# First chunk normed and turned tile by tile, mask copies on VectorE, and six output tiles moved among the second exp units

## The chip, the cores and the metric

The kernel runs on one core of a Trainium2 chip. The metric is device time in microseconds (us), as the median of several executions. The time is longer than the span of the profile, which runs from the first to the last instruction: by 1.8 us in the kernel before.

Engines are named as the profile names them: PE (TensorE matmul), PEld (its weight loads), DVE (VectorE), ACT (ScalarE), POOL (GpSimd), SP (SyncE). "SPq" is SyncE's queue, used here for DMA issues. L640 is line 640 of that kernel's own file, so one operation has different line numbers in different kernels.

## The reference, cut to what matters

```python
x = A_x                                    # 1 x 2048 x 512, bf16
xn = layernorm(x)
# branch A: 32 heads of 16, each query sees 8 keys at distance 0, 2, .., 14
qkv = xn @ wqkv;  attn = softmax(mask(q . k / 4));  s = (attn . v) @ wo
# branch B: LN, w1, gelu, shift in time by group, w2, residual, LN, w3, gelu, w4, residual
h  = gelu(layernorm(xn) @ w1);  x1 = xn + shift(h) @ w2
b  = x1 + gelu(layernorm(x1) @ w3) @ w4
out = x + s * silu(b)
```

Since the distances are even, even and odd tokens are two separate problems of 1024 tokens ("parity" p = 0, 1).

## The kernel before

Each parity is cut into nine attention units of up to 128 queries. The program has five stages:

1. The head: layer norm of four chunks of 512 tokens, their transposes, most q/k products and all w1 products.
2. The nine units of parity 0, filled with q/k and w2 products.
3. All of w3.
4. The nine units of parity 1, filled with w4 tiles.
5. The tail: the remaining w4 tiles, the gates, and 16 output tiles called `final_tile`.

Program order is issue order on each engine. These are the parts that the change and the argument touch.

```python
wm = psa("warm_ps")                        # warm-up of PE
for i in range(16):
    nc.tensor.matmul(wm[:, i % 2, :], lhsT=ones_bf[:], rhs=..., start=True, stop=True)
...
def mask_diag():                           # three column sums by VectorE
    nc.vector.tensor_tensor(out=tab[:, :, 0:P], in0=tab[:, :, 0:P], in1=ident..., op=ALU.mult)
    nc.vector.tensor_reduce(out=mg[:, 0:3], in_=tab[:, :, 0:P], ...)
def mask_rows():  ...                      # nine small operations, all on GpSimd
def mask_wide():  ...                      # two copies of 128x1024 on ScalarE
def mask_turn():                           # 2 x 16 matmuls of 64 columns, two copies on ScalarE
    ...
def mask_fill(k):                          # the mask into the queries and keys: four DMAs of 512 KB
    cs = slice(k * CH, (k + 1) * CH)
    for w in range(2):
        for e in range(2):
            nc.sync.dma_start(
                out=(kT, qT)[w][e][:, :, cs], in_=mask[:, w, cs].unsqueeze(1).to_broadcast([P, ND, CH]))
...
def rsqrt_eps(dst, var):                   # the inverse root of every layer norm: on GpSimd
    nc.gpsimd.tensor_scalar(out=dst, in0=var, scalar1=EPS, scalar2=None, op0=ALU.add)
    nc.gpsimd.tensor_tensor(out=dst, in0=dst, in1=nhalf[:, 0 : dst.shape[-1]], op=ALU.pow)
...
def final_tile(p, i, eng=nc.vector):
    pt = psa("wo_ps")[:, 0, :]
    for dt in range(ND):
        nc.tensor.matmul(pt, lhsT=oT[p][:, dt, i * P : (i + 1) * P], rhs=wo_sb[:, dt, :], ...)
    ...
    nc.vector.tensor_tensor(out=sg, in0=pt, in1=xn[p][:, i, :], op=ALU.mult)     # L638
    x_o = xo[p][:, i, :]
    eng.tensor_tensor(out=x_o, in0=sg, in1=x_o, op=ALU.add)                      # L640
...
    load_w3()
    va = values(0, 0)                      # value product of the first unit
    stage_w1(3, 0)
    stage_w1(3, 1)                         # last gelus, then ScalarE loads its exp table
...
    for n in range(N1, 2 * NU):            # nine units of parity 1, with w4 tiles 0 to 9
        attend(n)
    ...
    for t in range(10, 16):                # tail
        w4s[t](0, NF)
        final_tile(*fq.pop(0), eng=nc.gpsimd)
        gate(t)
        ...
    for _ in range(2):
        final_tile(*fq.pop(0), eng=nc.gpsimd)
    ...
    for i in range(8):
        final_tile(1, i, eng=nc.vector if i % 2 else nc.gpsimd)
        if i % 2:
            store(nc.scalar, 1, i - 1)
        if i == 2:
            normalise_end(1, 2)
```

The softmax here doesn't subtract the row's maximum and nothing guards it: scores larger than these inputs give would overflow.

Of the kernel before, what the change touches and what calls it, by code (L numbers as in the profile page):

```python
# [15 lines left out]
def kernel(  # L16
# [153 lines left out]
    def mask_tables():  # L170
        gp = nc.gpsimd
        for i, o, v in ((0, 0, -7), (0, 15, 8), (1, 1, -7), (1, 16, 7)):
            gp.iota(
                tab[:, i, o : o + 135].rearrange("p (k t) -> p k t", t=15)[:, ::2],
                pattern=[[0, 5], [1 if o < 15 else -1, 15]], base=v, channel_multiplier=0,
                allow_small_or_imprecise_dtypes=True,
            )
        gp.memset(tab[:, 1, 0:1], -8.0)
        gp.iota(
            tab[:, 2, 0:P].rearrange("p (g k) -> p g k", k=2), pattern=[[0, P // 2], [-2, 2]], base=1,  # L180
            channel_multiplier=0, allow_small_or_imprecise_dtypes=True,
        )
        for w in range(2):
            m = rows[w]
            gp.memset(m, 0.0)
            gp.memset(m[:, :, 3:11], PEN if w == 0 else 0.0)
            gp.affine_select(
                out=m[:, :, 3:11], in_=m[:, :, 3:11], pattern=[[-1, W], [1, W]],
                compare_op=ALU.is_ge if w == 0 else ALU.not_equal,
                fill=-PEN if w == 0 else 1.0, base=0, channel_multiplier=0,  # L190
            )
        gp.memset(rows[0][:, :, 2], -PEN)
        gp.memset(rows[1][:, :, 0], 1.0)

    def mask_diag():
        nc.vector.tensor_tensor(
            out=tab[:, :, 0:P], in0=tab[:, :, 0:P], in1=ident.unsqueeze(1).to_broadcast([P, 3, P]), op=ALU.mult
        )
        nc.vector.tensor_reduce(out=mg[:, 0:3], in_=tab[:, :, 0:P], axis=mybir.AxisListType.X, op=ALU.add)

    def mask_rows():
        gp = nc.gpsimd
        sg, q = mg[:, 2:3], mg[:, 3:4]
        one = ones_bf[:, 0:W]
        for w in range(2):
            m = rows[w]
            c, d = mg[:, w : w + 1], m[:, :, 3:11]
            gp.tensor_scalar(out=d, in0=d, scalar1=sg, scalar2=None, op0=ALU.mult)
            gp.tensor_scalar(out=q, in0=c, scalar1=-1.0 if w == 0 else 1.0, scalar2=c, op0=ALU.add, op1=ALU.mult)
            if w == 0:  # L210
                gp.tensor_scalar(out=q, in0=q, scalar1=1.0, scalar2=-PEN, op0=ALU.add, op1=ALU.mult)
                gp.tensor_scalar(out=m[:, :, 0], in0=one, scalar1=q, scalar2=None, op0=ALU.mult)
                gp.tensor_scalar(out=m[:, :, 1], in0=one, scalar1=c, scalar2=2 * PEN, op0=ALU.mult, op1=ALU.mult)
            else:
                gp.tensor_scalar(out=m[:, :, 1], in0=one, scalar1=c, scalar2=None, op0=ALU.mult)
                gp.tensor_scalar(out=m[:, :, 2], in0=one, scalar1=q, scalar2=None, op0=ALU.mult)

    def mask_wide():
        for w in range(2):
            nc.scalar.copy(  # L220
                out=wide[:, w, :].rearrange("p (l n r) -> p l n r", l=W, r=16),
                in_=rows[w].unsqueeze(2).to_broadcast([P, W, P // 16, 16]),
            )

    def mask_turn():
        for w in range(2):
            pt = psa("mask_ps").rearrange("p b x -> p (b x)")
            pv = pt.rearrange("p (b g l) -> p b l g", b=2, l=W)
            for b in range(2):
                for l in range(W):  # L230
                    nc.tensor.matmul(
                        pv[:, b, l, :], lhsT=wide[:, w, l * P : (l + 1) * P], rhs=ident[:, b * 64 : b * 64 + 64],
                        start=True, stop=True,
                    )
            nc.scalar.copy(out=mask[:, w, :], in_=pt)

    def mask_fill(k):
        cs = slice(k * CH, (k + 1) * CH)
        for w in range(2):
            for e in range(2):  # L240
                nc.sync.dma_start(
# [14 lines left out]
    for i in range(NV):  # L256
        va = const.tile([P, H, 2 * DH], BF16, name=f"v_aug{i}")
        nc.gpsimd.memset(va[:, :, DH : 2 * DH], 2.0)
        v_aug.append(va)

# [23 lines left out]
    def ln_stats(c, lo=0, hi=TPC):  # L284
        p, k = c // 2, c % 2
        lns.setdefault(c, []).append((lo, hi, *layer_stats(xn[p][:, k * TPC : (k + 1) * TPC, :], "l1", lo, hi)))

# [341 lines left out]
    def final_tile(p, i, eng=nc.vector):  # L629
        pt = psa("wo_ps")[:, 0, :]  # L630
# [7 lines left out]
        nc.vector.tensor_tensor(out=sg, in0=pt, in1=xn[p][:, i, :], op=ALU.mult)  # L638
# [13 lines left out]
    ln_stats(0, 0, 2)  # L652
    ln_stats(0, 2, 4)
    ln_norm(0)
    stage_t(0, 0)
    stage_t(0, 1)
    ln_again(0)
    mask_diag()
    mask_rows()
    ln_stats(1)  # L660
    ln_again(1)
    stage_d(0)
    ln_norm(1)
    parts = [qk_pair(0, a, 2) for a in range(2)]
    for hh in range(2):
        for f in parts:
            f[hh]()
    mask_wide()
    qk_pair(0, 2)[0]()
    stage_r(0)  # L670
    stage_m(0)
    qk_pair(0, 3)[0]()
    mask_turn()
    mask_fill(0)
    stage_t(1, 0)
    stage_t(1, 1)
    spread(0, 0, CH)
    mask_fill(1)
    ln_stats(2)
    ln_again(2)  # L680
    stage_w1(0, 0)
    stage_w1(0, 1)
    stage_d(1)
    ln_norm(2)
# [6 lines left out]
    spread(0, CH, M)  # L691
    stage_t(2, 0)
    stage_t(2, 1)
    ln_stats(3)
    ln_again(3)
    stage_d(2)
# [11 lines left out]
    stage_m(3)  # L708
    stage_w1(2, 0)
    stage_w1(2, 1)  # L710
    load_w3()
    va = values(0, 0)
    stage_w1(3, 0)
    stage_w1(3, 1)

# [10 lines left out]
    for n, (a, b) in enumerate(  # L726
        (("www", "q"), ("w", "qw"), ("w", "qq"), ("w", "qw"), ("w", "qq"), ("w", "qw"), ("w", "qq"), ("w", "qw"), ("w", "qw"))
# [20 lines left out]
    for n in range(N1, 2 * NU):  # L748
        t = n - N1
        if t == 0:  # L750
            groups[n][0].append(lambda: w4s[0](0, NF))
            groups[n][0].append(lambda: w4s[1](0, 5))
            groups[n][1].append(lambda: w4s[1](5, NF))
        else:
            groups[n][0].append(lambda t=t: gate(t - 1))
            groups[n][0].append(lambda t=t: w4s[t + 1](0, 5))
            groups[n][1].append(lambda t=t: w4s[t + 1](5, NF))
# [19 lines left out]
    def attend(n):  # L777
# [3 lines left out]
        out = weighted(*prev) if prev is not None else None  # L781
        for f in groups[n][0]:
            f()
# [4 lines left out]
        if out and n >= N1:  # L788
            out()
# [12 lines left out]
    for c in range(NCH):  # L802
        for a in range((NF + 1) // 2):
            w3_pair(c, a)
            if c == 0 and a == 0:
# [12 lines left out]
                load_w4()  # L818
                pack(0, 2)
# [6 lines left out]
    load_wo()  # L826
# [10 lines left out]
    fq = [(0, i) for i in range(8)]  # L837
    gate(8)
    gate(9)
    for t in range(10, 16):  # L840
        w4s[t](0, NF)
        final_tile(*fq.pop(0), eng=nc.gpsimd)
        gate(t)
        if t == 11:
            normalise_end(1, 1)
        if t == 13:
            normalise_mid(1, 2)
            normalise_rr(1, 2)
    for _ in range(2):
        final_tile(*fq.pop(0), eng=nc.gpsimd)  # L850
    for i in (0, 2, 4, 6):
        store(nc.sync, 0, i)
    for i in range(8):
        final_tile(1, i, eng=nc.vector if i % 2 else nc.gpsimd)
        if i % 2:
            store(nc.scalar, 1, i - 1)
        if i == 2:
            normalise_end(1, 2)
# [30 lines left out]
```

## Time and profile before

| What | Value | View |
|---|---|---|
| time | 217.96 us (217.96 to 217.99) | timed runs |
| span | 216.2 us | page |
| PE busy | 202.4 us, 94% | page |
| PE stops being the limit | 198.9 us | chain of waits |
| DVE's last add ends | 210.05 us | timeline |
| PE in the last 5 us before 210 | 2.50 of 5 us | table of windows |

First, two lines of the page's second part. Each digit is the busy share of one fortieth of the span.

```profile
PE   8999999999999999999999999999999999999830
POOL 8881505000054797902180000000610708534940
```

PE is full until slice 37. The loss is at the end. The table of windows shows the same place in finer steps: the window, its length, then the busy time of each engine with its number of instructions.

```profile
195.00:200.00 5.00, 4.62 (x21) 2.02 (x21) 4.91 (x5) 0.63 (x1) 2.22 (x2) 1.00 0.54 145
200.00:205.00 5.00, 4.03 (x18) 1.67 (x18) 4.97 (x8) 0.00 (x0) 4.66 (x4) 1.00 0.40 136
205.00:210.00 5.00, 2.50 (x11) 0.88 (x9) 4.90 (x8) 0.00 (x0) 2.84 (x3) 1.00 0.44 150
```

The first busy column is PE and the third is DVE. DVE is full (4.97, 4.90) while PE falls to half. The chain of waits, which is the work that ended last in order of time, agrees.

```profile
203.41 1.12 DVE arena L615
204.53 0.61 DVE arena L638
...
207.86 1.29 DVE arena L638 x2
209.15 0.02 issue
209.17 0.88 DVE arena L640
```

DVE's last add ends at 210.05, yet the span lasts to 216.2. The view of the program's closing line shows why. Its columns are the count, then the shortest, median and longest duration in ns, then the first and last start.

```profile
L884 POOLq DRAIN  x3: 40/102/6513, 208.6 to 215.6; - x3
L884 SPq DRAIN  x3: 7/7/13, 212.4 to 215.4; - x3
```

SyncE starts its closing at 212.4, when the last store has landed. GpSimd's first drain starts at 208.6 and lasts 6.51 us, to 215.1. The closing barrier comes only after that.

### The profile page before, as it was taken

The numbers are of one execution on the slowest core, as the hardware profiler recorded it, in microseconds if no ns is written. First come the engines' busy times: TensorE is split into PE (matmuls) and PEld (weight loads), VectorE is DVE, ScalarE is ACT, GpSimd is POOL, SyncE is SP. The second block draws the span as 40 slices with busy tenths as digits, with TensorE's granted clock in tenths as the row PEclk, the third lists the DMA queues.
The fourth block names the chain that finished last, engine by engine and source line by source line (L and its number), as shares of the span: only waits on it lengthen the run. The fifth ranks groups of instructions, "written<-read, shape, count | busy, mean of one in ns | idle before, by whom it ended". The sixth has DMA issues, their size and how long they took to land.

```text
span 216.2 us, 5001 instructions
## 1 busy us (share of the span) xinstructions
PE 202.4 (94%) x1999; PEld 98.9 (46%) x2028; DVE 132.8 (61%) x242; ACT 133.1 (62%) x162; POOL 78.1 (36%) x155
## 2 busy tenths in 40 slices
PE   8999999999999999999999999999999999999830
PEld 2557455444444444544444444445444444444310
DVE  4868686223788786867731000355667697799980
ACT  2378678859879888665665568788888861211000
POOL 8881505000054797902180000000610708534940
PEclk9999999999999999999999999999999999999995
DMA  5993977977401697772589766880210603105431
GB/s 134 359 349 113 322 110 166 312 115 144 188 5 20 159 171 101 160 171 48 151 200 201 235 128 98 254 264 0 53 33 4 138 15 79 57 0 136 151 115 49
DMA packets 34782, 29.75 MB, mean 138 GB/s; under 512 B 12600, under 2 KB 32408, under 8 KB 34760
## 3 DMA queue, kind: packets, MB, share of 16 engines
q1 hardware_dynamic: 31624, 25.24, 44.2%
q0 software_dynamic: 2048, 3.15, 8.9%
q10 hardware_dynamic: 1088, 1.05, 1.4%
q8 instruction: 16, 0.26, 0.5%
q14 instruction: 6, 0.05, 0.1%
HBM read 12.39 MB, written 4.46 MB: 78 GB/s over the span
## 4 chain that ended last, share of the span: by engine, by line
PE 79%; DVE 5%; ACT 5%; SPq 4%; issue 4%; DMA 1%; DVEq 0%
PE w_ps L458 18%; PE w_ps L478 17%; PE qk_ps L362 7%; PE v_ps L504 6%; PE s_ps L524 6%; PE w_ps L414 5%; SPq L250 4%; PE qk_ps L378 4%; PE o_ps L547 4%; PE wo_ps L632 3%; PE w_ps L391 3%; PE warm_ps L161 3%; DVE arena L638 3%; ACT arena L529 2%; PE tr_ps L314 1%
## 5 line engine op out<-in xcount | busy, mean ns | idle before, releaser
L529 ACT ACTIVATE arena<-s_ps 128x960 bf16<-128x960 f32 (+2 forms) x72 | 63.1, 934 | 15.8 <-PE s_ps L524 15.1
L589 POOL DMA_DIRECT2D arena<-orw x48 | 25.2, 532 | 61.6 <-DVE orw L559 61.6
L478 PE MATMUL w_ps<-arena 128*128 128x512 bf16 (+1 forms) x154 | 38.7, 379 | 0.7 <-issue 0.2
L463 ACT ACTIVATE arena<-w_ps 128x1024 bf16<-128x1024 f32 x20 | 20.5, 1024 | 15.6 <-PE w_ps L458 14.9
L458 PEld LDWEIGHTS <-arena 128*128 128x128 bf16 (+1 forms) x176 | 17.5, 100 | 20.2
L478 PEld LDWEIGHTS <-arena 128*128 128x128 bf16 (+1 forms) x176 | 16.5, 97 | 19.4 <-issue 0.4
L494 DVE SCALAR_TENSOR_TENSOR arena<-sig,arena 128x512 bf16<-128x512 bf16 x16 | 14.7, 926 | 14.2 <-ACT sig L493 14.1
L559 DVE CAST orw<-o_ps 128x960 bf16<-128x960 f32 (+2 forms) x18 | 19.7, 1095 | 1.4 <-PE o_ps L547 1.4
L493 ACT ACTIVATE sig<-arena 128x512 bf16<-128x512 bf16 x16 | 10.1, 630 | 16.2 <-DVE arena L484 16.2
L458 PE MATMUL w_ps<-arena 128*128 128x512 bf16 (+1 forms) x86 | 19.4, 379 | 0.1
L418 DVE TENSOR_TENSOR arena<-w_ps,arena 128x512 bf16<-128x512 f32 x16 | 11.0, 688 | 13.7 <-PE w_ps L414 13.6
L524 PEld LDWEIGHTS <-arena 32*128 32x128 bf16 (+1 forms) x576 | 11.8, 94 | 16.7 <-issue 16.2
L458 PE MATMUL w_ps<-arena,arena 128*128 128x512 bf16 (+1 forms) x86 | 19.1, 379 | 0.1
L640 POOL TENSOR_TENSOR arena<-arena 128x512 bf16<-128x512 bf16 x12 | 14.8, 1244 | 11.6 <-DVE arena L638 11.6
L524 PE MATMUL s_ps<-arena 32*128 32x120 bf16 (+2 forms) x576 | 18.5, 211 | 0.5 <-ACT arena L529 0.2
L504 PE MATMUL v_ps<-wv_sb,arena 128*128 128x512 bf16 (+1 forms) x71 | 18.5, 381 | 0.1
L362 PE MATMUL qk_ps<-arena 128*128 128x512 bf16 (+1 forms) x95 | 18.2, 343 | 0.2
L266 POOL TENSOR_SCALAR l3r<-l3m 128x1 f32<-128x1 f32 (+1 forms) x10 | 2.3, 229 | 41.3 <-DVE l3m L275 41.3
L414 PE MATMUL w_ps<-arena 128*128 128x512 bf16 x55 | 15.6, 381 | 0.6 <-issue 0.2
L508 DVE CAST v_aug<-v_ps 128x512 bf16<-128x512 f32 (+1 forms) x18 | 12.4, 687 | 4.9 <-PE v_ps L504 4.9
L484 DVE TENSOR_TENSOR arena<-w_ps,arena 128x512 bf16<-128x512 f32 x16 | 10.9, 680 | 6.8 <-PE w_ps L478 6.7
L391 PE MATMUL w_ps<-arena 128*128 128x512 bf16 x61 | 14.3, 379 | 0.2
(83 smaller groups left out, 262.7 us busy)
## 6 DMA issues: line engine op xcount, KB each, us to landing
arena<-arena SPq DMA_DIRECT2D x8, 512.0 KB, 5.6
arena<-arena SPq DMA_DIRECT2D x48, 64.0 KB, 2.5
x1n_dram<-arena SPq DMA_DIRECT2D x4, 512.0 KB, 4.3
arena<-in_A_x_dram SPq DMA_DIRECT2D x4, 512.0 KB, 8.0
arena<-in_A_x_dram SPq DMA_DIRECT2D x6, 256.0 KB, 7.0
arena<-in_B_w_dram SPq DMA_DIRECT2D x1, 1376.0 KB
arena<-in_B_w_dram SPq DMA_DIRECT2D x1, 1280.0 KB
arena<-in_A_wqkv_dram SPq DMA_DIRECT2D x2, 512.0 KB, 4.4
```

The lines of the kernel that those rows point to most:

```text
L362: nc.tensor.matmul(pt[:, b, hh * w : (hh + 1) * w], lhsT=wqk_sb[:, dt, nt * P : (nt + 1) * P], rhs=xnT[p][:, dt, k * CH + hh * w : k * CH ...
L391: nc.tensor.matmul(pt[:, b, :], lhsT=w1_sb[:, dt, g * P : (g + 1) * P], rhs=xn2T[c][:, dt, :], start=(dt == 0), stop=(dt == ND - 1),)
L414: nc.tensor.matmul(pt, lhsT=w2_src(p, g, m0), rhs=w2_sb[:, g, :], start=(g == 0), stop=(g == ND - 1))
L458: nc.tensor.matmul(pt[:fs, ft % 2, :], lhsT=w3_sb[:, dt, ft * P : ft * P + fs], rhs=x1nT[c][:, dt, :], start=(dt == 0), stop=(dt == ND - 1),)
L463: nc.scalar.activation(h3(c, 2 * a, 2), pt, AF.Gelu_apprx_tanh)
L478: nc.tensor.matmul(pt, lhsT=h3(c, ft, 1)[:fs, 0, jj * P : (jj + 1) * P], rhs=w4_sb[:fs, ft, :], start=(ft == 0), stop=(ft == NF - 1),)
L504: nc.tensor.matmul(vp[:nk, :], lhsT=xnT[p][:, dt, k0 : k0 + nk], rhs=wv_sb[:, dt, :], start=(dt == 0), stop=(dt == ND - 1),)
L524: nc.tensor.matmul(st[:nk, b, i * nq : (i + 1) * nq], lhsT=kT[e][r : r + 32, dt, k0 : k0 + nk], rhs=qT[e][r : r + 32, dt, q0 : q0 + nq], s ...
L529: nc.scalar.activation(prv[:nk, 2 * h : 2 * h + 2], st[:nk, :, 0 : 4 * nq], AF.Exp, scale=SCALE)
L559: nc.vector.tensor_copy(out=orw[p][:, :, :, q0 - ra : q0 - ra + nq], in_=op[:, :, 0 : 4 * nq].rearrange("p j (s q) -> p j s q", q=nq),)
L589: nc.gpsimd.dma_start(out=oT[p][DH * hh : DH * (hh + 1), :, ra : ra + rw], in_=orw[p][32 * cg : 32 * cg + DH, jj],)
L640: eng.tensor_tensor(out=x_o, in0=sg, in1=x_o, op=ALU.add)
```

## The change

The change has three parts:

- **Head.** Chunk 0 is normed and turned one tile at a time. The mask's column sums move from VectorE to PE, its turn becomes 16 transposes, and its widening and eight copies move from ScalarE and DMA to VectorE. Part of its small operations move from GpSimd to VectorE, and the statistics of chunks 1 and 3 are taken in halves.
- **Units.** The value product of the first unit moves behind the last w1 products, and one more q/k product goes into that unit. Six output tiles of parity 0 move into units 2 and 6 of parity 1, and two fewer w4 tiles are done there.
- **Tail.** Seven of the eight w4 tiles each carry one output tile and three output tiles follow the last w4 tile; all adds of the tail are on VectorE, and the last store is 128 KB.

```diff
+    def mask_cols():                       # replaces mask_diag
+        pt = pst("w", "mask_ps")[:, 0, 0:3]
+        for i in range(3):
+            nc.tensor.matmul(pt[:, i : i + 1], lhsT=tab[:, i, 0:P], rhs=ident[:, 0:1], start=True, stop=True)
+        nc.scalar.copy(out=mg[:, 0:3], in_=pt)
...
+    def mask_turn(w):
+        pt = psa("mask_ps").bitcast(BF16)
+        for l in range(W):
+            nc.tensor.transpose(pt[:, w, l * P : (l + 1) * P], wide[:, w, l * P : (l + 1) * P], ident[:])
...
     def mask_fill(k):
         ...
-                nc.sync.dma_start(
+                nc.vector.tensor_copy(
                     out=(kT, qT)[w][e][:, :, cs], in_=mask[:, w, cs].unsqueeze(1).to_broadcast([P, ND, CH])
...
+    parts = [qk_pair(0, a, 2) for a in range(3)]     # head, in the new order
+    parts[0][0]()
+    ...
+    mask_cols()
+    mask_rows(0, nc.gpsimd)
+    ln_stats(1, 0, 2)
...
+    stage_d(1)
+    mask_fill(0)
+    spread(0, 0, CH)
     ln_norm(2)
...
     load_w3()
-    va = values(0, 0)
     stage_w1(3, 0)
     stage_w1(3, 1)
+    va = values(0, 0)
...
+    fill = {0: (0, 1), 1: (2,), 3: (3,), 4: (4,), 5: (5,), 7: (6,), 8: (7,)}   # w4 tiles by unit
+    rows_of = {2: (0, 1, 2), 6: (3, 4, 5)}                                     # output tiles by unit, adds on GpSimd
...
-    for t in range(10, 16):
+    fq = [(0, 6), (0, 7)] + [(1, i) for i in range(8)]
+    for t in range(8, 16):
         w4s[t](0, NF)
-        final_tile(*fq.pop(0), eng=nc.gpsimd)
...
+        if t < 15:
+            p, i = fq.pop(0)
+            final_tile(p, i, ps=psa)       # add on VectorE
+            gate(t)
...
+    final_tile(1, 5, ps=psa, act=True)     # act: ScalarE copies the product out of PSUM first
+    store(nc.sync, 1, 4)
+    gate(15)
+    final_tile(1, 6, ps=psa, act=True)
+    store(nc.sync, 1, 6, 1)
+    final_tile(1, 7, ps=psa)
+    store(nc.scalar, 1, 7, 1)
```

More of the change, by code (lines that the diff above doesn't have):

```diff
@@ L182, in mask_tables @@
         )
-        for w in range(2):
-            m = rows[w]
-            gp.memset(m, 0.0)
-            gp.memset(m[:, :, 3:11], PEN if w == 0 else 0.0)
-            gp.affine_select(
-                out=m[:, :, 3:11], in_=m[:, :, 3:11], pattern=[[-1, W], [1, W]],
-                compare_op=ALU.is_ge if w == 0 else ALU.not_equal,
-                fill=-PEN if w == 0 else 1.0, base=0, channel_multiplier=0,
-            )
-        gp.memset(rows[0][:, :, 2], -PEN)
-        gp.memset(rows[1][:, :, 0], 1.0)
@@ L195, in mask_diag @@
-    def mask_diag():
-        nc.vector.tensor_tensor(
-            out=tab[:, :, 0:P], in0=tab[:, :, 0:P], in1=ident.unsqueeze(1).to_broadcast([P, 3, P]), op=ALU.mult
-        )
-        nc.vector.tensor_reduce(out=mg[:, 0:3], in_=tab[:, :, 0:P], axis=mybir.AxisListType.X, op=ALU.add)
-    def mask_rows():
-        gp = nc.gpsimd
+    def mask_cols():
[3 more added lines that the diff above has]
+        nc.scalar.copy(out=mg[:, 0:3], in_=pt)
@@ new lines, in mask_forms @@
+    def mask_forms(w):
+        gp = nc.gpsimd
+        m = rows[w]
+        gp.memset(m, 0.0)
+        gp.memset(m[:, :, 3:11], PEN if w == 0 else 0.0)
+        gp.affine_select(
+            out=m[:, :, 3:11], in_=m[:, :, 3:11], pattern=[[-1, W], [1, W]],
+            compare_op=ALU.is_ge if w == 0 else ALU.not_equal,
+            fill=-PEN if w == 0 else 1.0, base=0, channel_multiplier=0,
+        )
+        if w == 0:
+            gp.memset(m[:, :, 2], -PEN)
+        else:
+            gp.memset(m[:, :, 0], 1.0)
@@ L203, in mask_rows @@
+    def mask_rows(w, eng):
         sg, q = mg[:, 2:3], mg[:, 3:4]
         one = ones_bf[:, 0:W]
-        for w in range(2):
-            m = rows[w]
-            c, d = mg[:, w : w + 1], m[:, :, 3:11]
-            gp.tensor_scalar(out=d, in0=d, scalar1=sg, scalar2=None, op0=ALU.mult)
-            gp.tensor_scalar(out=q, in0=c, scalar1=-1.0 if w == 0 else 1.0, scalar2=c, op0=ALU.add, op1=ALU.mult)
-            if w == 0:
-                gp.tensor_scalar(out=q, in0=q, scalar1=1.0, scalar2=-PEN, op0=ALU.add, op1=ALU.mult)
-                gp.tensor_scalar(out=m[:, :, 0], in0=one, scalar1=q, scalar2=None, op0=ALU.mult)
-                gp.tensor_scalar(out=m[:, :, 1], in0=one, scalar1=c, scalar2=2 * PEN, op0=ALU.mult, op1=ALU.mult)
-            else:
-                gp.tensor_scalar(out=m[:, :, 1], in0=one, scalar1=c, scalar2=None, op0=ALU.mult)
-                gp.tensor_scalar(out=m[:, :, 2], in0=one, scalar1=q, scalar2=None, op0=ALU.mult)
+        m = rows[w]
+        c, d = mg[:, w : w + 1], m[:, :, 3:11]
+        eng.tensor_scalar(out=d, in0=d, scalar1=sg, scalar2=None, op0=ALU.mult)
+        eng.tensor_scalar(out=q, in0=c, scalar1=-1.0 if w == 0 else 1.0, scalar2=c, op0=ALU.add, op1=ALU.mult)
+        if w == 0:
+            eng.tensor_scalar(out=q, in0=q, scalar1=1.0, scalar2=-PEN, op0=ALU.add, op1=ALU.mult)
+            eng.tensor_scalar(out=m[:, :, 0], in0=one, scalar1=q, scalar2=None, op0=ALU.mult)
+            eng.tensor_scalar(out=m[:, :, 1], in0=one, scalar1=c, scalar2=2 * PEN, op0=ALU.mult, op1=ALU.mult)
+        else:
+            eng.tensor_scalar(out=m[:, :, 1], in0=one, scalar1=c, scalar2=None, op0=ALU.mult)
+            eng.tensor_scalar(out=m[:, :, 2], in0=one, scalar1=q, scalar2=None, op0=ALU.mult)
@@ L218, in mask_wide @@
     def mask_wide():
         for w in range(2):
-            nc.scalar.copy(
+            nc.vector.tensor_copy(
                 out=wide[:, w, :].rearrange("p (l n r) -> p l n r", l=W, r=16),
@@ L223, in mask_wide @@
             )
-    def mask_turn():
-        for w in range(2):
-            pt = psa("mask_ps").rearrange("p b x -> p (b x)")
-            pv = pt.rearrange("p (b g l) -> p b l g", b=2, l=W)
-            for b in range(2):
-                for l in range(W):
-                    nc.tensor.matmul(
-                        pv[:, b, l, :], lhsT=wide[:, w, l * P : (l + 1) * P], rhs=ident[:, b * 64 : b * 64 + 64],
-                        start=True, stop=True,
-                    )
-            nc.scalar.copy(out=mask[:, w, :], in_=pt)
+    def mask_turn(w):
+        pt = psa("mask_ps").bitcast(BF16)
+        for l in range(W):
+            nc.tensor.transpose(pt[:, w, l * P : (l + 1) * P], wide[:, w, l * P : (l + 1) * P], ident[:])
+        nc.scalar.copy(
+            out=mask[:, w, :].rearrange("p (g l) -> p g l", l=W), in_=pt[:, w, :].rearrange("p (l g) -> p g l", l=W)
+        )
     def mask_fill(k):
@@ L240, in mask_fill @@
             for e in range(2):
-                nc.sync.dma_start(
+                nc.vector.tensor_copy(
                     out=(kT, qT)[w][e][:, :, cs], in_=mask[:, w, cs].unsqueeze(1).to_broadcast([P, ND, CH])
@@ L257, with v_ones @@
         va = const.tile([P, H, 2 * DH], BF16, name=f"v_aug{i}")
-        nc.gpsimd.memset(va[:, :, DH : 2 * DH], 2.0)
         v_aug.append(va)
+    def v_ones():
+        for va in v_aug:
+            nc.gpsimd.memset(va[:, :, DH : 2 * DH], 2.0)
     for p in range(2):
@@ L286, in ln_stats, with ln_first, first_n, first_t @@
         lns.setdefault(c, []).append((lo, hi, *layer_stats(xn[p][:, k * TPC : (k + 1) * TPC, :], "l1", lo, hi)))
+    first = {}
+    def ln_first(j):
+        if not first:
+            first["st"] = small.tile([P, TPC, nc.vector.BN_STATS_DIM], F32, name="l0s", tag="l0s", bufs=1)
+            first["mv"] = small.tile([P, TPC, nc.vector.BN_AGGR_DIM], F32, name="l0m", tag="l0m", bufs=1)
+            first["r"] = small.tile([P, TPC], F32, name="l0r", tag="l0r", bufs=1)
+            lns[0] = [(0, TPC, first["mv"], first["r"])]
+        st, mv, rstd = first["st"], first["mv"], first["r"]
+        nc.vector.bn_stats(out=st[:, j, :], in_=xn[0][:, j, :])
+        nc.vector.bn_aggr(out=mv[:, j, :], in_=st[:, j, :])
+        r = rstd[:, j : j + 1]
+        nc.vector.tensor_scalar(out=r, in0=mv[:, j, 1:2], scalar1=EPS, scalar2=None, op0=ALU.add)
+        nc.gpsimd.tensor_tensor(out=r, in0=r, in1=nhalf[:, 0:1], op=ALU.pow)
+    def first_n(j):
+        mv, rstd = first["mv"], first["r"]
+        nc.vector.tensor_scalar(
+            out=xn[0][:, j, :], in0=xn[0][:, j, :], scalar1=mv[:, j, 0:1],
+            scalar2=rstd[:, j : j + 1], op0=ALU.subtract, op1=ALU.mult,
+        )
+    def first_t(j):
+        pt = pst("wb"[j % 2], "tr_ps").bitcast(BF16)[:, 0, 0:CH].rearrange("p (a q) -> p a q", a=ND)
+        for dt in range(ND):
+            nc.tensor.transpose(pt[:, dt, :], xn[0][:, j, dt * P : (dt + 1) * P], ident[:])
+        nc.scalar.copy(out=xnT[0][:, :, j * P : (j + 1) * P], in_=pt)
     def ln_norm(c):
@@ L627, in load_xo, with final_tile @@
         )
-    def final_tile(p, i, eng=nc.vector):
-        pt = psa("wo_ps")[:, 0, :]
+    def final_tile(p, i, eng=nc.vector, ps=psb, act=False):
+        pt = ps("wo_ps")
+        if ps is psa:
+            pt = pt[:, 0, :]
         for dt in range(ND):
@@ L637, in final_tile @@
         sg = at(75 + cnt["g"] % 4, 1, D)[:, 0, :]
-        nc.vector.tensor_tensor(out=sg, in0=pt, in1=xn[p][:, i, :], op=ALU.mult)
+        if act:
+            nc.scalar.copy(out=sg, in_=pt)
+        nc.vector.tensor_tensor(out=sg, in0=sg if act else pt, in1=xn[p][:, i, :], op=ALU.mult)
         x_o = xo[p][:, i, :]
@@ L651 @@
     mask_tables()
-    ln_stats(0, 0, 2)
-    ln_stats(0, 2, 4)
-    ln_norm(0)
-    stage_t(0, 0)
-    stage_t(0, 1)
-    ln_again(0)
-    mask_diag()
-    mask_rows()
-    ln_stats(1)
-    ln_again(1)
-    stage_d(0)
-    ln_norm(1)
-    parts = [qk_pair(0, a, 2) for a in range(2)]
-    for hh in range(2):
-        for f in parts:
-            f[hh]()
-    mask_wide()
-    qk_pair(0, 2)[0]()
+    ln_first(0)
+    ln_first(1)
+    mask_forms(0)
+    first_n(0)
+    first_t(0)
+    ln_first(2)
+    mask_forms(1)
+    first_n(1)
+    first_t(1)
+    parts = [qk_pair(0, a, 2) for a in range(3)]
+    parts[0][0]()
+    ln_first(3)
+    first_n(2)
+    first_t(2)
+    parts[1][0]()
+    first_n(3)
+    first_t(3)
+    parts[2][0]()
+    ln_again(0)
+    mask_cols()
+    mask_rows(0, nc.gpsimd)
+    ln_stats(1, 0, 2)
+    stage_d(0)
+    ln_stats(1, 2, 4)
+    ln_again(1)
+    v_ones()
+    parts[0][1]()
     stage_r(0)
     stage_m(0)
+    ln_norm(1)
+    mask_rows(1, nc.vector)
+    mask_wide()
+    parts[1][1]()
+    parts[2][1]()
     qk_pair(0, 3)[0]()
-    mask_turn()
-    mask_fill(0)
+    stage_w1(0, 0)
     stage_t(1, 0)
     stage_t(1, 1)
-    spread(0, 0, CH)
-    mask_fill(1)
     ln_stats(2)
     ln_again(2)
-    stage_w1(0, 0)
     stage_w1(0, 1)
+    mask_turn(0)
+    mask_turn(1)
     stage_d(1)
+    mask_fill(0)
+    spread(0, 0, CH)
     ln_norm(2)
@@ L690 @@
         qk_pair(1, a)[0]()
-    spread(0, CH, M)
     stage_t(2, 0)
     stage_t(2, 1)
-    ln_stats(3)
+    ln_stats(3, 0, 2)
+    stage_d(2)
+    ln_stats(3, 2, 4)
     ln_again(3)
-    stage_d(2)
     ln_norm(3)
@@ L708 @@
     stage_m(3)
+    mask_fill(1)
+    spread(0, CH, M)
     stage_w1(2, 0)
@@ L726 @@
     for n, (a, b) in enumerate(
-        (("www", "q"), ("w", "qw"), ("w", "qq"), ("w", "qw"), ("w", "qq"), ("w", "qw"), ("w", "qq"), ("w", "qw"), ("w", "qw"))
+        (("www", "qq"), ("w", "qw"), ("w", "qq"), ("w", "qw"), ("w", "qq"), ("w", "qw"), ("w", "qq"), ("w", "qw"), ("w", "w"))
     ):
@@ L747 @@
     w4s = [w4_tile(t) for t in range(S // P)]
-    for n in range(N1, 2 * NU):
-        t = n - N1
-        if t == 0:
-            groups[n][0].append(lambda: w4s[0](0, NF))
-            groups[n][0].append(lambda: w4s[1](0, 5))
-            groups[n][1].append(lambda: w4s[1](5, NF))
-        else:
-            groups[n][0].append(lambda t=t: gate(t - 1))
-            groups[n][0].append(lambda t=t: w4s[t + 1](0, 5))
-            groups[n][1].append(lambda t=t: w4s[t + 1](5, NF))
+    fill = {0: (0, 1), 1: (2,), 3: (3,), 4: (4,), 5: (5,), 7: (6,), 8: (7,)}
+    rows_of = {2: (0, 1, 2), 6: (3, 4, 5)}
+    ready = ()
+    for k in range(NU):
+        a, b = groups[N1 + k]
+        gates = [lambda t=t: gate(t) for t in ready]
+        ready = fill.get(k, ())
+        if ready:
+            a += gates
+            if len(ready) == 2:
+                a.append(lambda t=ready[0]: w4s[t](0, NF))
+            t = ready[-1]
+            a.append(lambda t=t: w4s[t](0, 5))
+            b.append(lambda t=t: w4s[t](5, NF))
+        else:
+            i0, i1, i2 = rows_of[k]
+            a.append(lambda i=i0: final_tile(0, i, nc.gpsimd))
+            a.append(lambda i=i1: final_tile(0, i, nc.gpsimd))
+            a += gates
+            b.append(lambda i=i2: final_tile(0, i, nc.gpsimd))
     for p in range(2):
@@ L781, in attend @@
         out = weighted(*prev) if prev is not None else None
+        if out and n >= N1:
+            out()
         for f in groups[n][0]:
@@ L787, in attend @@
         prs.append(scores(p, u, 1))
-        if out and n >= N1:
-            out()
         if N1 <= n < len(order) - 1:
@@ L818 @@
                 load_w4()
+                load_wo()
                 pack(0, 2)
@@ L825 @@
                 normalise_end(0, 2)
-    load_wo()
     for k in range(2):
@@ L836 @@
     normalise_dn(1, 2)
-    fq = [(0, i) for i in range(8)]
-    gate(8)
-    gate(9)
-    for t in range(10, 16):
+    gate(7)
+    for i in (0, 2, 4):
+        store(nc.sync, 0, i)
+    fq = [(0, 6), (0, 7)] + [(1, i) for i in range(8)]
+    for t in range(8, 16):
         w4s[t](0, NF)
-        final_tile(*fq.pop(0), eng=nc.gpsimd)
-        gate(t)
         if t == 11:
             normalise_end(1, 1)
-        if t == 13:
+        if t == 14:
+            normalise_end(1, 2)
+        if t < 15:
+            p, i = fq.pop(0)
+            final_tile(p, i, ps=psa)
+            gate(t)
+            if i % 2:
+                store(nc.sync, p, i - 1)
+        if t == 10:
             normalise_mid(1, 2)
             normalise_rr(1, 2)
-    for _ in range(2):
-        final_tile(*fq.pop(0), eng=nc.gpsimd)
-    for i in (0, 2, 4, 6):
-        store(nc.sync, 0, i)
-    for i in range(8):
-        final_tile(1, i, eng=nc.vector if i % 2 else nc.gpsimd)
-        if i % 2:
-            store(nc.scalar, 1, i - 1)
-        if i == 2:
-            normalise_end(1, 2)
+    final_tile(1, 5, ps=psa, act=True)
[5 more added lines that the diff above has]
+    store(nc.scalar, 1, 7, 1)
 _INS = ['A_x', 'A_wqkv', 'A_wo', 'B_x', 'B_w1', 'B_w2', 'B_w3', 'B_w4']
```

## The prediction

> **What bounds the kernel now.** In the timeline and the chain of waits TensorE is the limit from 7.2 us (end of the 16 warm-up matmuls) to 198.9 us: the chain stays on PE, and 16 matmuls of 512 columns take 3.45 us, back to back. After 198.9 it is VectorE: PE is busy 2.50 of 5 us in 205–210, and the chain walks along DVE `wo` products (0.68 us), adds (0.65–0.88) and a normalising product (1.12) until 210.05. The last store lands near 212.4, yet the span ends at 216.2: SyncE is done at 212.5, and GpSimd, whose last add starts at 208.6, shows one drain of 6.5 us until 215.1; the closing barrier takes 1.05 more. Time is 1.76 us over the span.
>
> **The change, costed.**
> 1. Mask turn: 32 matmuls (1.79 us in the chain) become 16 transposes (16 take 0.89): −0.9 us of PE. Three one-column matmuls: +0.2.
> 2. First chunk: warm-up still holds PE until 7.22, so the first qk starts about 0.25 us earlier (9.10 before), and 8 transposes that were done by then (0.45) come later: +0.2.
> 3. Eight 512 KB mask DMAs become VectorE copies of 2048 bf16. None is in this trace; the Trainium skill, "VectorE: DVE Perf Modes", perf-mode tier table, has 693 ns for that size: an estimate of 5.5 us more DVE. DVE idles over 2 us in each 10 us there, but layer-norm waits tighten: around 24–37 us I take +0.5 of PE stall.
> 4. Value matmuls after the last gelu and one more qk in the first unit hide table load and exps (second scores there take 0.90 us instead of 0.34): −0.6.
> 5. Six finals among the second exp units, adds on GpSimd. Units are 4.95 us, PE-bound with 0.25 of waiting for exps, which units with three finals lack: −0.3. GpSimd adds slow VectorE's products of two SBUF inputs (0.69 alone, 1.62 beside one); buffers should absorb it. The skill's "GPSIMD Engine Reference", Specifications, says the SBUF interfaces are shared; this trace agrees.
> 6. Tail: eight w4 tiles (2.38 us of PE) each with a final (0.86): 3.24 us of PE against about 2.5 of DVE (0.68+0.68+0.69, and an add near 0.42 with GpSimd silent, estimated from 1.226 for 2048 elements). PE stays the limit to its end. At 198.9 there remain 28 `wo` matmuls, 6.05 us: PE would end at 204.9 less the gains of 1–5 (0.9): 204.0. Then 2.9 us of sums, gates and adds: DVE ends near 206.9, against 210.05.
> 7. GpSimd's last work is now the packing early in the tail, so its drain is hidden; from the last DVE add to the end 3.3 us (issue 0.45, landing 1.7, barrier) rather than 6.15.
>
> Span 206.9 + 3.3 = 210.2; time **212.0 us**, range 209.8 to 215.2. About 6 us go: 3 from a PE-bound tail, 2.8 from the hidden drain. Faster by over 2% (below 213.6): 0.77; within 2%: 0.22; slower: 0.01.
>
> **What would show it.** Right: PE tenths of 9 until about 204 us; tail adds near 0.42; GpSimd drain ended before the last store lands; mask turn near 0.9; exp units near 4.95; mask copies near 0.7 without new PE gaps at 24–40 us. Wrong: a GpSimd drain that still ends 2–3 us after the last store (time near 214.8: the largest single risk); PE gaps at 30–37 us behind layer norm; units with finals over 5.5 us; PE waiting for the third normalisation at the end.
>
> **What would make it wrong.** VectorE copies at half speed (about 1.2 us, 4 us more); PSUM buffers held longer by VectorE in the exp units; or the drain being of fixed place rather than fixed length.

## The result, and the profile after

The median is 211.9 us (211.42 to 212.17, four runs) against 217.97 us. The ratio is 0.9719, with a 95% interval of 0.9701 to 0.9737. The profiled span is 209.4 us; it is that of the fastest of the four runs, and the other three span 209.8 to 210.1 us.

These are the lines of the kernel after that answer to those of before: the busy slices, the windows, the end of the chain, and the closing.

```profile
PE   8899999799999999999999999999999999999990
POOL 6878557200032889921163000001840392700000
```

```profile
195.00:200.00 5.00, 4.94 (x24) 2.27 (x24) 3.76 (x7) 1.20 (x2) 0.00 (x0) 1.00 0.18 59
200.00:205.00 5.00, 4.44 (x21) 1.81 (x19) 3.93 (x9) 1.65 (x4) 0.00 (x0) 1.00 0.00 0
```

```profile
200.99 0.86 PE w_ps L507 x4
201.85 0.88 PE wo_ps L663 x4
...
205.65 0.61 DVE arena L671
206.26 0.02 issue
206.28 0.43 DVE arena L673
```

```profile
L947 POOLq DRAIN  x3: 40/102/6721, 181.8 to 209.1; - x3
L947 SPq DRAIN  x3: 7/7/13, 208.6 to 208.9; - x3
```

PE now stays full to about 204.4 us and DVE is no longer full. DVE's last add ends at 206.71. GpSimd's long drain starts at 181.8 and is over by 188.5, so SyncE's closing at 208.6 is followed at once by the barrier. From the last add to the end there are 2.7 us (209.4 − 206.71), where there were 6.15 before.

The slices also show something new: a 7 in PE's eighth slice, 36.6 to 41.9 us. The list of PE's waits has one of 1.1 us there, and the timelines of GpSimd and VectorE show where it begins.

```profile
PE rrep_ps L368 <- DVE arena L361: 1.1, 1, 1.1
```

```profile
23.46 3.45 POOL L268 TENSOR_TENSOR l1r<-l1r,nhalf 128x4 f32<-128x4 f32 x1
...
36.88 1.04 POOL L268 TENSOR_TENSOR r<-r,nhalf 128x4 f32<-128x4 f32 x1
```

```profile
23.52 2.49 DVE L239 COPY arena<-arena 128x2048 bf16<-128x2048 bf16 x4
26.94 0.73 DVE L322 TENSOR_SCALAR arena<-arena,l1m,l1r 128x512 bf16<-128x512 bf16 x2 [0.93 <-POOL l1r L268]
```

The same power of 128x4 takes 1.04 us at 36.88 but 3.45 us while VectorE runs its four mask copies. The extra 2.4 us are as long as the copies (2.49 us). VectorE's next layer norm had to wait for that power. From there the chain stays on VectorE and GpSimd until 38.75 us, where PE starts `rrep_ps` again.

### The profile page after: what moved, and what is told of

Read it like the earlier page. It is cut to its first block, busy times and chain, and to the rows that moved or that the text cites. A ratio compares the mean times of both kernels' runs of the same rounds, so it can differ in the third digit from the quotient of the medians.

```text
span 209.4 us, 5001 instructions
## 1 busy us (share of the span) xinstructions
PE 199.6 (95%) x1994; PEld 98.3 (47%) x2023; DVE 137.2 (66%) x264; ACT 133.5 (64%) x163; POOL 76.3 (36%) x151
## 4 chain that ended last, share of the span: by engine, by line
PE 82%; DVE 8%; POOL 6%; issue 2%; ACT 1%
PE w_ps L507 18%; PE w_ps L487 18%; PE v_ps L533 8%; PE s_ps L553 7%; PE w_ps L443 7%; PE wo_ps L663 6%; PE qk_ps L407 5%; PE o_ps L576 4%; PE w_ps L420 3%; POOL l1r L268 3%; PE warm_ps L161 3%; DVE l1s L275 2%; PE qk_ps L391 1%; DVE arena L322 1%; DVE arena L361 1%
## 5 line engine op out<-in xcount | busy, mean ns | idle before, releaser
L673 POOL TENSOR_TENSOR arena<-arena 128x512 bf16<-128x512 bf16 x6 | 7.7, 1299 | 45.8 <-DVE arena L671 45.8
L553 PE MATMUL s_ps<-arena 32*128 32x120 bf16 (+2 forms) x576 | 17.6, 211 | 0.0
L644 DVE TENSOR_TENSOR arena<-arena,orw 128x1440 bf16<-128x1440 bf16 (+1 forms) x2 | 1.7, 842 | 20.6 <-DMA orw<-rden_d 20.6
```

The source lines that it names most:

```text
L553: nc.tensor.matmul(st[:nk, b, i * nq : (i + 1) * nq], lhsT=kT[e][r : r + 32, dt, k0 : k0 + nk], rhs=qT[e][r : r + 32, dt, q0 : q0 + nq], s ...
```

## The experiments

Theories:

- **D**: the end of the kernel before waits for GpSimd's drain, which has a fixed length after GpSimd's last instruction.
- **S**: the new head gives nothing, because VectorE's mask copies stop GpSimd and layer norm waits for GpSimd.

Rivals:

- **F**: what follows the last add is fixed, whatever GpSimd does.
- **G/H**: the head carries a real part of the gain.
- **V**: PE's new wait comes from VectorE's own extra work.

All twelve runs are told. The kernels of one group ran together on one chip: the first four, the second four and the last four (the last two groups on the same chip).

### 1. The old tail with its adds on VectorE (b_dve_adds)

```diff
-        final_tile(1, i, eng=nc.vector if i % 2 else nc.gpsimd)
+        final_tile(1, i, eng=nc.vector)
```

> The kernel before, with one word changed: the last eight output tiles' adds are all on VectorE, none on GpSimd. Theory D (the end of the kernel before waits for GpSimd's drain, which lasts about 5.4 us after GpSimd's last instruction): GpSimd's last add now ends near 201.5 us, its drain near 207, so it is hidden; VectorE ends about where it did (four adds of 0.42 us more, four others quicker without GpSimd beside them: near 210.3), and the end follows it by about 3.0 us: span 213.3, time about 215.1, ratio 0.987. Rival F (the 6.15 us from the last add to the end are fixed by the last store and the closing, whatever GpSimd does): time 218.2, ratio 1.001.

Measured: 216.25 us (215.97 to 216.29), ratio 0.9917, interval 0.9903 to 0.9932. That is a saving of 1.7 us where D expected 2.9 and F a loss of 0.2. The two terms of D's sum have to be read apart.

```profile
L884 POOLq DRAIN  x3: 40/102/7025, 200.9 to 213.9; - x3
L884 SPq DRAIN  x3: 7/7/13, 213.4 to 213.7; - x3
```

```profile
L640 DVE TENSOR_TENSOR arena<-arena x8: 425/425/1394, 201.5 to 210.6; 128x512 bf16<-128x512 bf16 x8
```

The drain ended at 207.9, well before SyncE's closing at 213.4. From VectorE's last add (210.61 + 0.42 = 211.03) to the end of the span (214.2) there are 3.2 us instead of 6.15, so D's own term came nearly as expected (3.0). Of the 1.2 us that are missing, 0.2 are this, 0.7 are VectorE's, which ended later than I had put it, and 0.3 lie outside the span (the time is 2.06 us over it here and 1.76 before), which is not explained. In its timeline seven of the eight adds took 0.42 or 0.43 us, but one took 1.39 us (from 201.47), while GpSimd's last two adds ran (200.32 to 202.58). That one is about 1 us over the rest.

### 2. A tiny GpSimd copy at the end of the kernel after (a_touch5, a_touch7)

```diff
     final_tile(1, 7, ps=psa)
     store(nc.scalar, 1, 7, 1)
+    tch = small.tile([P, 1], BF16, name="tch", tag="tch", bufs=1)
+    nc.gpsimd.tensor_copy(out=tch, in_=xo[1][:, 5, 0:1])      # a_touch7: row 7
```

> The kernel after, with one GpSimd copy of a single column at the very end, which reads output tile (1,5) after its add (ends at 204.25 us); nobody reads what it writes. Theory D: the drain runs from about 204.4 to 209.8 us, and the closing of 1.05 us ends the span near 210.9 instead of 209.4: about 213.3 us of time, ratio 0.979. Rival F: as the kernel after, 211.9 us, ratio 0.972.

> The same copy, but of output tile (1,7), whose add is VectorE's last instruction (ends at 206.71 us). Theory D: drain from about 206.9 to 212.3, span near 213.3, time about 215.8, 3.9 us over the kernel after, ratio 0.990. Rival F: as the kernel after, ratio 0.972 (at most 0.973).

Measured: 213.90 us (ratio 0.9814, interval 0.9800 to 0.9829) and 215.64 us (ratio 0.9888, interval 0.9869 to 0.9906). Both are within 0.3% of what D said, and F is refuted. The closing lines show it, first for tile 5, then for tile 7.

```profile
L949 POOLq DRAIN  x3: 40/102/5930, 205.0 to 211.4; - x3
L949 SPq DRAIN  x3: 7/7/13, 209.3 to 211.2; - x3
```

```profile
L949 POOLq DRAIN  x3: 40/102/5535, 207.4 to 213.4; - x3
L949 SPq DRAIN  x3: 7/7/13, 209.2 to 213.2; - x3
```

SyncE is ready at 209.3 and 209.2. The drain ends at 210.9 and 212.9, and the span follows it (211.7 and 213.7). The copies end at 205.60 and 207.57 in the timelines, so the drain ends 5.3 to 5.4 us after them. In the kernel before, the last GpSimd add ends at 209.77 and the drain at 215.1, which is 5.3 us again. One copy of a single column, whose result nobody reads, costs this kernel up to 3.7 us. In the traces, 0.7 and 0.6 us of the longer span are not the drain's: VectorE's last add itself starts at 206.98 and 206.89 instead of 206.28 us, since the warm-up of PE took longer in these two executions (run 7).

### 3. The second half alone (b_tail)

The edit is the kernel before with only the new units of parity 1, the new tail and the earlier load of `wo`. The head and the first unit are as before.

> The kernel before with only the second half of the change: six finals among the second exp units, the new tail, the weights of the output product loaded earlier. The first half (mask, first chunk, first unit) as before. Theory: the first half is worth only the 0.84 us by which the first-phase units end earlier in the trace after, so time is about 212.7 us, ratio 0.976. Rival H (the first half gives more, because what it frees helps later stages too): above 214, ratio over 0.982.

Measured: 212.26 us (212.19 to 212.27), ratio 0.9736, interval 0.9722 to 0.9751. Of the 6.1 us, 5.7 come from these parts.

### 4. The head alone (b_head)

The edit is the kernel before with the new chunk 0, the new mask and its copies on VectorE. The value product stays where it was, and units and tail are the old ones.

> The kernel before with only the first part of the change: first chunk tile by tile, the mask by transposes, its copies by VectorE; the value product of the first unit stays ahead of the last w1 pairs, the first unit has one qk, and the tail is the old one. In the trace after, PE is 1.1 us ahead at the first qk and loses it again: 1.05 us of waiting at 37.7 us for GpSimd's second inverse root. Theory S (GpSimd is stopped while VectorE runs the mask copies, one power there took 3.45 us instead of 1.05): the head gives nothing, 0.0 to -0.4 us, ratio 0.998 to 1.000. Rival G (the head is the source of the 0.84 us at the end of the first units): 217.1 us, ratio 0.996 or less.

Measured: 218.19 us (218.09 to 218.66), ratio 1.0016, interval 1.0003 to 1.0029. The head alone gains nothing and costs about 0.2 us. Its trace has the stretched power (3.46 us at 23.51) and a PE wait of 1.3 us before `rrep_ps`. Its first scores start at 47.18 us against 46.51 before.

### 5. The value product alone (b_values)

```diff
     load_w3()
-    va = values(0, 0)
     stage_w1(3, 0)
     stage_w1(3, 1)
+    va = values(0, 0)
...
-        (("www", "q"), ("w", "qw"), ... ("w", "qw"), ("w", "qw"))
+        (("www", "qq"), ("w", "qw"), ... ("w", "qw"), ("w", "w"))
```

> The kernel before with only the value product moved behind the last w1 pairs and one more qk in the first unit (one less in the last). Theory: the table load and the first exps are then covered, PE's second scores fall from 0.90 to 0.35 us and the first units end 0.8 to 1.2 us earlier: 216.8 to 217.2 us, ratio 0.995 to 0.996. Rival G: no more than 0.3 us, ratio 0.9985 or more.

Measured: 216.78 us (216.77 to 216.81), ratio 0.9945, interval 0.9932 to 0.9957. The gain is 1.2 us, at the upper edge of what the theory gave. The chain of waits of this run stays on PE through the table load, and the second scores take 0.35 us where PE had shown 0.90 us before:

```profile
49.70 0.86 PE v_ps L504 x4
50.56 0.35 PE s_ps L524 x16
50.92 1.83 PE qk_ps L378 x8
```

### 6. The mask copies back on DMA (a_fill0_dma, a_fill01_dma)

The edit is the kernel after with `mask_fill(0)`, or both calls, in the old DMA form. In the second kernel `mask_fill(1)` stands behind the first spreading, as it did before.

> The kernel after, with the first half of the mask copies (four of the eight) back on DMA, at the same place; the second half stays on VectorE. Theory S: the power on GpSimd beside them takes 1.05 us again instead of 3.45, layer norm of chunk 2 starts near 24.8 instead of 26.9, PE does not wait at 37.7 us (1.05 us): up to 1.0 us less than the kernel after, ratio about 0.967. Rival V (the wait comes from VectorE's own extra work and order in 28 to 37 us): the wait stays, ratio 0.971 to 0.972.

> The kernel after, with all eight mask copies back on DMA, the second four right behind the first spreading as in the kernel before. Theory S: the same as with the first four alone, since GpSimd is idle while the second four run: ratio about 0.967. If the copies' DMA share costs anything later (weights for w3, spreading), ratio above that of the first four alone.

Measured: 210.88 us (210.54 to 211.58, ratio 0.9676, interval 0.9659 to 0.9692) and 210.94 us (210.44 to 211.37, ratio 0.9676, interval 0.9662 to 0.9689). Each is about 1.0 us under the kernel after, and they are equal to each other. So only the first four copies cost anything. The power beside them is back to its length, and VectorE's layer norm of chunk 2 starts at 24.99 instead of 26.94:

```profile
23.91 1.04 POOL L276 TENSOR_TENSOR l1r<-l1r,nhalf 128x4 f32<-128x4 f32 x1
```

PE's wait before `rrep_ps` is gone from the list of waits. Rival V as it was put is out: in 28 to 37 us VectorE has the same operations and order in both kernels, and the wait is gone in one. But V has a stronger form, since the four copies also occupy VectorE for 2.49 us. The traces allow an estimate. The start of VectorE's four small products (22.89 us in the kernel after, 23.34 here) lies before the copies. From there to the layer norm of chunk 2 it takes 4.05 us with the copies and 1.65 without, 2.40 us more. The copies end at 26.01 us and the layer norm starts at 26.94, when the power is done. So about 1.5 of the 2.40 us are VectorE's own time, and about 0.9 are the stop of GpSimd.

There is a second stop, nearer to PE's wait. These are the kernel after (two lines) and a_fill0_dma:

```profile
35.21 1.22 DVE L375 TENSOR_TENSOR arena<-arena 128x2048 bf16<-128x2048 bf16 x1
35.42 1.06 POOL L332 TENSOR_TENSOR r<-r,l1m 128x2 f32<-128x2 f32 x1
```

```profile
34.16 0.20 POOL L340 TENSOR_TENSOR r<-r,l1m 128x2 f32<-128x2 f32 x1
```

The same small product of GpSimd takes 1.06 us while VectorE multiplies two SBUF inputs, and 0.20 us when it does not. In the kernel after it stands in the chain that ends with PE's wait, so an estimate gives it 0.86 of the 1.05 us. In b_head GpSimd's last two such products take 1.50 and 0.19 us instead of 0.36 and 1.06, 0.27 us more, and PE's wait is longer by as much (1.3 us). The one edit of this run took away the copies' time and both stops. So it shows that the copies cost about 1.0 us, but not which of the three would have cost PE its wait alone. Theory S is right as to the loss and only in part as to its cause.

### 7. The kernel after again (a_same)

> The kernel after, unchanged, beside the others on this chip: 211.9 us, ratio 0.972. Its executions should scatter by some 0.3% as before, where the kernel before repeats within 0.05%: the warm-up matmuls' length (5.54 us in its trace, 5.5 to 6.5 in the other traces) now moves the mask's column sums, which GpSimd waits for.

Measured: 211.95 us (211.24 to 212.39), ratio 0.9723, interval 0.9706 to 0.9741. It repeats, and it scatters by 0.5%, while eight of the nine runs of the kernel before beside it lie between 217.94 and 217.99 us. The warm-up took 6.00 us in this trace and 5.54 in the first one. The first q/k product moved with it; these are the timelines of the kernel after, then of this run.

```profile
1.05 5.54 PE L161 MATMUL warm_ps<-ones_bf 128*128 128x512 bf16 x16 [1.05 <-DVE arena L264]
...
8.00 1.03 PE L391 MATMUL qk_ps<-arena 128*128 128x256 bf16 x8 [0.67 <-ACT arena L315]
```

```profile
1.04 6.00 PE L161 MATMUL warm_ps<-ones_bf 128*128 128x512 bf16 x16 [1.04 <-DVE arena L264]
...
8.43 1.03 PE L391 MATMUL qk_ps<-arena 128*128 128x256 bf16 x8 [0.94 <-ACT arena L315]
```

The two profiled executions took 211.42 and 211.86 us: 0.46 us more warm-up, 0.43 later at the first q/k, 0.44 us more time. The traces of run 2 agree: warm-ups of 6.28 and 6.19 us, 0.74 and 0.65 more than 5.54, and last adds 0.70 and 0.61 us later. In the old head the first q/k starts at 9.10 or 9.09 us whether the warm-up took 5.48 (b_values), 6.17 (before) or 6.29 us (b_tail_values), since PE waits there for VectorE's layer norm.

### 8. The change without its head (b_tail_values)

The edits of 3 and 5 together.

> The change without its head: old first chunk, old mask with its DMA copies, but the value product behind the last w1 pairs, one more qk in the first unit, six finals among the second exp units, the new tail. Theory S (the head as it stands costs, since GpSimd's layer-norm steps wait for it): the parts add up, -1.2 and -5.7 us, time about 211.1 us, 0.8 us under the kernel after, ratio 0.968. Rival G (the head carries part of the gain): at or above the kernel after, ratio 0.972 or more.

Measured: 211.08 us (211.07 to 211.11), ratio 0.9684, interval 0.9671 to 0.9697. The parts add up to a tenth of a microsecond, and this kernel is 0.9 us faster than the full change on the same chip. It also repeats within 0.04 us. The head, then, costs the full change 0.9 us.

That is more than the 0.2 us that it costs alone, and the traces show a part of why. First scores of the first unit, then of the tenth, are at 46.51 and 131.81 us (before) against 47.18 and 132.17 us (head alone). About 0.3 us of the delay is swallowed by the waits in the old first unit. With the value product moved there is nothing to swallow it: 46.50 and 130.63 us without the head, 47.27 and 131.40 us with it (a_same). The rest of the 0.7 us between the two costs is not explained; the profiled run of b_head (218.59 us) was 0.4 us over its median.

Where the 0.77 us come from can be read off too. From its first q/k to the first scores PE is busy 37.41 us without the head and 37.56 us with it (a table of windows, 9.09 to 46.50 and 8.43 to 47.27 us), but it never idles without the head and idles 1.28 us with it. The head starts 0.66 us earlier, then adds 1.28 us of waits, and saves PE no work.

### 9. GpSimd's mask rows behind the inverse roots (a_rows_later)

```diff
-    mask_rows(0, nc.gpsimd)
     ln_stats(1, 0, 2)
     stage_d(0)
     ln_stats(1, 2, 4)
+    mask_rows(0, nc.gpsimd)
     ln_again(1)
```

> The kernel after, with GpSimd's first mask rows (2.1 us in its trace, 11.58 to 13.64) moved behind the two inverse roots of chunk 1, mask copies still on VectorE. Theory S names two stops in one serial line of VectorE and GpSimd, the mask rows and the 3.45 us power: taking out the first should shorten PE's wait of 1.05 us at 37.7 us by about half to all of it: 211.0 to 211.5 us, ratio 0.968 to 0.970, and less scatter. If the 3.45 us power alone sets the wait: no change, ratio 0.972.

Measured: 211.61 us (211.03 to 212.25), ratio 0.9708, interval 0.9688 to 0.9729. The median is 0.34 us better than that of a_same, but the intervals overlap and the scatter stays, so this is inconclusive as to time. The traces say more once the warm-up is taken out: the first scores of the tenth unit less the length of the warm-up are 125.00 us here, against 125.39 to 125.43 in the four traces of the unchanged head (after, a_same, a_touch5, a_touch7). So the move is worth about 0.4 us, less than half of PE's wait, which fell only from 1.1 to 0.8 us. The chain no longer goes through the mask rows: it goes from the warm-up over the transposes of chunk 1 to the copies and the 3.46 us power. Taking one stop out put another in its place.

### 10. Fewer warm-up matmuls (a_fill0_warm12)

The edit is a_fill0_dma with `range(12)` in place of `range(16)` at the warm-up.

> The kernel after with the first four mask copies on DMA (210.9 us when run alone) and 12 warm-up matmuls instead of 16. With the GpSimd stall gone, PE is the limit from the end of the warm-up (7.08 us in that trace) on, and tile 0 is normed at 5.36, tile 1 at 6.76: transposes and first qk can start about 0.6 us earlier, unless PE's matmuls then stay at their slow start (0.34 to 0.43 us each against 0.216) for longer. Expected 210.3 us, ratio 0.965; if the slow start only moves into the real work, no gain: ratio 0.967 to 0.969.

Measured: 210.49 us (210.42 to 210.55), ratio 0.9656, interval 0.9643 to 0.9669. This is the fastest kernel: it beats both the kernel before and the kernel after. The first q/k starts at 7.97 us, half a microsecond before that of a_fill0_dma (8.46). PE now waits 0.8 us for layer norm before its second tile, so the warm-up no longer sets the pace, and the four times lie within 0.13 us. The two kernels ran in different groups and the gain of 0.4 us is small; their intervals overlap slightly.

## Why the prediction was right

The time was forecast at 212.0 us and measured at 211.9. Agreement to 0.1 us is luck. The sum of the gains came as forecast (6.0 us), because the head's miss of 0.9 us was made up by the value product (0.6 us more than forecast) and by the last terms (0.3 us more). What is not luck is that the two largest terms, the tail and the drain, came by the mechanism that was forecast. Here it is point by point. Where two kernels are subtracted, both are of one group.

| Term of the prediction | Forecast | Measured |
|---|---|---|
| head: mask turn, first chunk, mask copies (1 to 3) | −0.9 + 0.2 + 0.2 + 0.5 = 0.0 us | +0.2 alone, +0.9 within the change |
| value product and one q/k (4) | −0.6 us | −1.2 us |
| six output tiles, tail, drain (5 to 7) | −5.4 us (6.0 less 0.6) | −5.7 us |
| end of PE | 204.0 us | 204.4 us |
| last VectorE add ends | 206.9 us | 206.71 us |
| from there to the end of the span | 3.3 us | 2.7 us |

**The tail was right.** A w4 tile with an output tile takes PE 3.24 us (for instance 179.16 to 182.40 in the chain); there are seven of these and not eight. VectorE's adds fall to 0.42 or 0.43 us when GpSimd is silent, as estimated. The units with output tiles take 5.03 and 4.90 us, near 4.95.

**The drain was right in mechanism and nearly in size.** It was the largest single risk, and runs 1 and 2 show it: SyncE stands ready, the drain ends 5.3 to 5.4 us after GpSimd's last instruction, and the end follows it. The forecast gave 3.3 us after the last add; there are 2.7.

**The value product was mis-sized by half.** I took only the second scores' wait (0.90 instead of 0.34 us). In the chains of before and of b_values PE reaches the same scores at 55.71 and 55.70 us, but the latter has one more q/k product behind it, so that product (four matmuls, 0.86 us at full pace) fitted into waits and costs nothing. A further 0.3 us comes from the next unit: the scores at 66.06 us before stand at 65.74, since two waits called "issue" (0.30 and 0.82 us, near 61 us) are gone.

**The head was wrong, in its sum and in its parts.** Its forecast was 0.0 us and it cost 0.9 within the change. PE did reach the first q/k 0.7 to 1.1 us earlier, not 0.25, in part since the warm-up was shorter in those two traces (6.00 and 5.54 us) than the 6.17 us that I took as fixed. But PE's stall was 1.1 us, not 0.5. The step that was mis-sized is item 3, "layer-norm waits tighten": I counted only VectorE's longer queue. I had applied the sharing of the SBUF interfaces in one direction alone, GpSimd slowing VectorE. In this head it works the other way: VectorE's copies hold GpSimd, and GpSimd computes the root that VectorE needs next. By the estimates under run 6 this takes 0.9 us at the copies and 0.86 us at a later product, beside 1.5 us of VectorE's own queue. The Trainium skill, "SBUF — State Buffer", Who interferes with whom, states this: copies in a two-port mode contend with GpSimd, and the loser blocks fully. This trace agrees that GpSimd is held, with 3.45 us instead of 1.04; who is held first is another matter (last section).

**The copies' own length was right.** The Trainium skill, "VectorE: DVE Perf Modes", perf-mode tier table, gives 693 ns for this size; the eight copies took 685 ns on average.

**The scatter was not foreseen.** The new head starts when the warm-up ends, and the warm-up's 16 matmuls took 5.48 to 6.46 us from trace to trace. The Trainium skill, "TensorE: Matmul & The Clock Gate", What's actually happening, says that the clock's window runs freely, so that the change to full speed falls differently in each run. The lengths here agree with that; no run here shows the window itself.

**What stays open.** The 5.7 us of run 3 were not split by a run into the six moved tiles, the PE-bound tail and the drain. In the traces the last add ends 3.3 us earlier (210.05 to 206.71) and the end follows it 3.45 us sooner (6.15 to 2.7). A split of the head into its parts was not run either. So whether its transposes alone, with the mask left as it was, would keep their gain is not shown. Runs 6 and 8 bound it: with the first copies mended the head is worth about 0.2 us (210.88 against 211.08, from different groups and not clear of the scatter of 210.54 to 211.58), and with 12 warm-up matmuls 0.6 us (210.49 against 211.08, one group).

## What to carry to other kernels

Look at what each engine does after the last store has landed. An engine that closes slowly after its last instruction should get that instruction early, and here a one-word change of engine was worth 1.7 us. When work moves to VectorE to relieve another engine, check who shares its ports and whether the next VectorE step needs that engine's result. Test the parts of a bundle alone: here two parts carry the whole gain and the third costs 0.9 us, which the good total hid.

## What the Trainium skill lacked or had wrong

- No page has GpSimd's closing drain, so far as I found: it ends 5.3 to 5.4 us after GpSimd's last compute instruction in four traces (before, b_dve_adds, a_touch5, a_touch7), and 6.0 us after its last DMA issue in the kernel after (182.51 to 188.5). It is in the open unless that instruction comes early enough.
- "SBUF — State Buffer" says that whoever starts first gets the shared pair. Here the power is recorded as starting at 23.46 us and the first of four copies at 23.52, yet the power lasted through all four (3.45 us against 1.04) and the copies ran at full speed (2.49 us for four). Spans on GpSimd are rough, so the order of two starts 0.06 us apart isn't certain. That a run of copies back to back holds GpSimd for the whole run, not for one instruction, is what the page lacks.
- "TensorE: Matmul & The Clock Gate" calls the cold start's cost small and variable. That is not wrong here (0.44 of 212 us), but in the new head, which starts at the end of the warm-up, it is most of the scatter that was seen between two profiled executions (211.42 and 211.86 us), and it hid a gain of 0.4 us in run 9.
